# Two-dimensional spectral mixer with backward pass: a negated spectrum in place of negated sine tables, and four smaller edits of the schedule

## The chip, the cores and the metric

The kernel runs on one core of a Trainium2 chip. The core has a matrix engine (TensorE, "PE" in the profile, with its weight loads as "PEld"), two elementwise engines that can read the matrix engine's accumulators in PSUM (VectorE, "DVE", and ScalarE, "ACT"), a third one that works in SBUF here (GpSimd, "POOL"), and a queue that issues transfers (SyncE, "SP"). The metric is device time in microseconds of one execution.

## The reference

```python
def _A_ref(x, w_r, w_i):                       # spectral filter
    X = rfft2(x.astype(float32)); X = X * (w_r + 1j*w_i)
    return irfft2(X, s=(S, D)).astype(bfloat16)
def _B_ref(x, w1, b1, w2, b2):                 # token-mixing MLP
    h = _layernorm(x)
    u = gelu(einsum("bsd,sf->bdf", h, w1) + b1)
    return (einsum("bdf,fs->bds", u, w2) + b2).transpose(0, 2, 1)
h  = x + _A_ref(_layernorm(x), w_r, w_i)
h2 = h + _B_ref(_layernorm(h), w1, b1, w2, b2)
# outputs: h2, and the gradients of x, w_r, w_i, w1, b1, w2, b2 for grad_out
```

S is 2048 tokens, D 448 features, F 1792 hidden units, all data bfloat16, one batch.

## The kernel before, in words

The two-dimensional transform is done by matmuls. Along the features it is one product with a cosine and sine table (`csF`); along the 2048 tokens it is split in two steps, 16 x 128: a row step (`row_a`, `row_b`), a transfer that reshuffles partitions (`D2`), and a block step with sine and cosine tables per block (`Ut`, `Vt`, and their transposes `UTt`, `VTt` for the inverse). The program runs through these stages:

1. Forward rows (lines 856 to 888). For each of 16 rows `t`: layer-norm statistics (`ln_stats`), an inverse standard deviation on GpSimd (`newton_gp`, ten dependent operations for a group of rows), a row matrix scaled by it (`scale_R`), the row matmuls, and the evacuation of their PSUM banks. Between them a generator (`gen_UV`) builds the tables, three steps a row; it stops for the row when it yields `True`.
2. Forward spectrum (`s2_stage`, called in line 912). For each of 16 blocks `g`, two to a round: three matmuls make the complex spectrum, `w_mult` multiplies it by the filter, and some rounds later `s2_inv` makes the inverse block.
3. Inverse rows, then the MLP forward and backward (lines 920 to 1178). The backward rows of the spectral part run inside the last MLP loop with a lag of three, `rows(t - LAG)`; the last ones follow in lines 1251 to 1254.
4. Backward spectrum (`s2_stage`, line 1259): the same, with four more products a round for the filter gradient, and no lag between spectrum and product.
5. Inverse rows of the backward pass with the layer-norm gradient of x (`gx_consumer`), and the remaining stores.

The order of TensorE, VectorE, ScalarE and SP is written out by the program; GpSimd's is chosen by the compiler's scheduler. Two devices set the order. `fill(n)` takes `n` steps from a list of pending generators, so that matmuls of another part stand between dependent ones: the gradient of the hidden layer (`dg_gen`) in the forward part, the weight gradients (`gw_gen`) in the backward part. `gw_gen` has 14 steps for 16 matmul slots, with four evacuations, their stores and, once in 28 steps, a transposing load. `drain()` runs what is left. `evac` copies a PSUM bank to SBUF, on ScalarE or VectorE: a planner (`Meter`) keeps a load for each of the two, adds an estimate for every operation, and `evac` takes the engine that would be done first. After each operation the smaller load is raised to the larger one minus a slack:

```python
low = max(self.load) - Meter.slack
self.load[0], self.load[1] = max(low, self.load[0]), max(low, self.load[1])
```

Both PSUM pools (`ps_ff` for the transform, `ps_mm` for filling matmuls) have four banks, used in turn.

Subtraction inside an accumulating matmul needs one operand negated. The kernel before negates tables: `gen_neg` writes `-Ut` into `Un` and `-UTt` into `UTn` on VectorE, once for the forward and once for the backward stage.

Of the kernel before, what the change touches and what calls it, by code (L numbers as in the profile page):

```python
# [13 lines left out]
ALU = mybir.AluOpType  # L14
ACT = mybir.ActivationFunctionType
# [23 lines left out]
N_FILL_F = (6, 3, 20, 3, 24, 2)  # L39
N_FILL_B = (16, 16, 40, 8, 24, 8)  # L40
INV_SD = 1.0 / float(S * D)
# [9 lines left out]
class Meter:  # L51


    slack = 2.0
    side = ()
# [14 lines left out]
    def __getattr__(self, name):  # L70
        fn = getattr(self.eng, name)

        def run(**kw):
            ap = kw["in_"] if "in_" in kw else kw["in0"]
            n = int(np.prod(ap.shape[1:]))
            self.load[self.i] += self.cost(name, n, ap.dtype == BF16)
            low = max(self.load) - Meter.slack
            self.load[0], self.load[1] = max(low, self.load[0]), max(low, self.load[1])
            fn(**kw)  # L79
# [40 lines left out]
def kernel(  # L120
# [26 lines left out]

    Meter.slack = 2.0
    ctx.enter_context(tc.block(schedule_with_timeline_sim=True))
# [303 lines left out]
    def gen_UV():  # L453
# [18 lines left out]
        for dst, o0, o1, pt in ((Ut, ou, ou, pu), (Vt, ov0, ov1, pv)):  # L472
# [7 lines left out]
            yield  # L480
            yield True
            comp = comp_ring.next()
# [104 lines left out]
    p_ring = ring(rS, 1808, 2, 2, 2, KW)  # L587
    Y_ring = ring(rS, 3616, 2, 2, 2, KW)
    aT_ring = ring(rAT, 0, 2, 4, P)
    D2 = cut(r2, 0, NG, 2, KW)  # L590
    Un = [r448[:, (NG + g) * P:(NG + g + 1) * P] for g in range(12)] + [rE[:, (3 * NT + g) * P:(3 * NT + g + 1) * P] for g in range(4)]
    UTn = cut(r448, 0, NG, P)
    cs_ring = ring(r452, 0, 4, 2, 2, KW)
# [64 lines left out]
    def s2_stage(get_x, on_mult, ml, n_fill, gap, make_inv, after_fwd=None, scale=None):  # L658
        flush()
        nh = NG // 2  # L660
        xs, ys = {}, {}

        lag = 2 + ml
        for c2 in range(nh + lag):
            if c2 < nh:
                xs[c2] = get_x(c2)
                if make_inv and c2 < 4:
                    gen_inv_s(4 + c2)
                    if c2 in (1, 2):
                        gen_inv_d(c2 - 1)  # L670
            for i in range(2):
                if make_inv and c2 >= 3:
                    next(wp, None)
                    next(wp, None)
                if c2 < nh:
                    g = 2 * c2 + i
                    px = ps_ff()
                    pv = px[:, 0:452].rearrange("p (c k) -> p c k", c=2)
                    mm(pv, lhsT=Vt[:, g, :], rhs=D2[:, g, :, :], start=True, stop=False)
                    mm(pv[:, 0, :], lhsT=Ut[:, g, :], rhs=D2[:, g, 1, :], start=False, stop=False)  # L680
                    mm(pv[:, 1, :], lhsT=Un[g], rhs=D2[:, g, 0, :], start=False, stop=True)
                    evac(out=xs[c2][:, i, :, :], in_=pv, scale=scale)
                if c2 >= lag:
                    s2_inv(2 * (c2 - lag) + i, ys[c2 - lag][:, i, :, :])
                if after_fwd is not None and c2 < nh and g % 4 == 3:
                    after_fwd(g // 4)
                fill(n_fill)
            if ml <= c2 < nh + ml:
# [5 lines left out]
    def gen_neg(dst, src):  # L694
        ve.tensor_scalar(out=dst, in0=src, scalar1=-1.0, scalar2=None, op0=ALU.mult)

    def w_mult(c2, xc, Wv, conj):
# [8 lines left out]
        ve.tensor_tensor(out=y[:, :, 0, :], in0=p1[:, :, 1, :], in1=p2[:, :, 0, :],  # L706
                         op=(ALU.subtract if conj else ALU.add))
        return y

    def s2_inv(g, y):  # L710
        pu = ps_ff()
        pv = pu[:, 0:452].rearrange("p (c k) -> p c k", c=2)
        mm(pv, lhsT=VTt[:, g, :], rhs=y, start=True, stop=False)
        mm(pv[:, 0, :], lhsT=UTt[:, g, :], rhs=y[:, 1, :], start=False, stop=False)
        mm(pv[:, 1, :], lhsT=UTn[:, g, :], rhs=y[:, 0, :], start=False, stop=True)
        ab = r452_ring.next()
# [46 lines left out]
    def ln_stats(src, t, mv):  # L763
        ve.bn_stats(out=stats[:, t, :], in_=src[:, t, :])
        if t % 2:
            ve.bn_aggr(out=mv[:, t - 1, :], in_=stats[:, t - 1, :])
        if t % 2:
            ve.bn_aggr(out=mv[:, t, :], in_=stats[:, t, :])

    def load_biases():  # L770
# [71 lines left out]
    for t in (4, 5):  # L842
        ln_stats(xn, t, mvx)
    newton_gp(mvx[:, 4:6, 1], rstd_x[:, 4:6], slice(4, 6))
    fill(6)
    turn_biases = load_biases()
    Meter.side, Meter.every, Meter.count = [], 1, 0
    GROUPS = {0: (6, 8), 1: (8, 10), 3: (10, 12), 5: (12, 14), 7: (14, 16)}
    STATS = {0: (6, 7), 1: (8, 9), **{t: (t + 8,) for t in range(2, 8)}}
    INV_S = {11: 0, 12: 1, 13: 2, 14: 3}  # L850
    for c in range(2):
        sc.copy(out=Rp.rearrange("p (a q b c) -> p c a q b", c=2, q=8, a=4)[:, c],
                in_=Rm[:, 64 * c:64 * c + 64].rearrange("p (q a b) -> p a q b", q=8, a=4))
    FILL_A = (3, 3, 3, 3, 3, 3, 3, 3, 3, 3, 3, 3, 3, 3, 3, 3)
    FILL_B = (3, 3, 3, 3, 3, 3, 3, 3, 3, 3, 3, 3, 3, 3, 3, 3)
    for t in range(NT):
        if t in (1, 3):
            load_w2T()
        if t + 1 < NT:
            row_a(t + 1, Rs.pop(t + 1))  # L860
        fill(FILL_A[t])
        if 1 <= t and t + 3 < NT:
# [19 lines left out]
        if t in INV_S:  # L882
            gen_inv_s(INV_S[t])
        if t in (13, 13 + 1):
            gen_neg((cut(r448, NG * P, 12, P), cut(rE, 3 * NT * P, 4, P))[t - 13], Ut[:, 12 * (t - 13):12 + 4 * (t - 13), :])
        if t == 2:
            gen_RT()
        fill(FILL_B[t])
    for i in range(2):
        gen_neg(UTn[:, 8 * i:8 * i + 8, :], UTt[:, 8 * i:8 * i + 8, :])  # L890
    wp = w_place()
    gp_.memset(csF[:, 0, :, 0:1], 1.0)
    fill(20)

# [16 lines left out]

    s2_stage(fwd_x, fwd_mult, ML_F, 3, 24, True)
    drain()
# [225 lines left out]

    for i in range(2):  # L1140
        gen_neg(cut(r2, (2 * NG * KW + 8 * i * P), 8, P), Ut[:, 8 * i:8 * i + 8, :])
    Un[:] = [r2[:, 2 * NG * KW + g * P:2 * NG * KW + (g + 1) * P] for g in range(NG)]
    LAG = 3
# [116 lines left out]
    Meter.slack = 2.0  # L1260
    g_out = w_io(W_view_B, out_2, out_3, True)
# [69 lines left out]
```

## Time and profile before

| what | value |
|---|---|
| three runs | 368.6, 369.4, 369.41 us, median 369.4 |
| the profiled execution's own time | 369.41 us |
| its span, first to last instruction | 367.6 us |
| TensorE busy | 346.1 us (94%) |
| VectorE, ScalarE, GpSimd busy | 255.8, 203.7, 73.7 us |
| chain of work that ended last | TensorE 77%, VectorE 6%, GpSimd 5%, transfers 4%, ScalarE 4% |
| transfers, share of 16 engines | 90.3% for the one hardware queue that carries nearly all |

A row of the wait list reads: engine, tile and line that waited, who released it, then the total wait in us, how often, and the longest. A row of the busy times by stretch reads: the stretch from the span's start, its length, then busy time and number of instructions of PE, PEld, DVE, ACT and POOL, the granted share of TensorE's clock, the share of the transfer engines, and GB/s. A row of a timeline reads: start, time, engine, line, operation, output, input, shape, and how many like instructions were merged; in brackets the idle time before it and who ended it. L79 is the planner's wrapper through which all VectorE and ScalarE operations go, and L215 the wrapper of all matmuls.

### The profile page before, as it was taken

The numbers are of one execution on the slowest core, as the hardware profiler recorded it, in microseconds if no ns is written. First come the engines' busy times: TensorE is split into PE (matmuls) and PEld (weight loads), VectorE is DVE, ScalarE is ACT, GpSimd is POOL, SyncE is SP. The second block draws the span as 40 slices with busy tenths as digits, with TensorE's granted clock in tenths as the row PEclk, the third lists the DMA queues.
The fourth block names the chain that finished last, engine by engine and source line by source line (L and its number), as shares of the span: only waits on it lengthen the run. The fifth ranks groups of instructions, "written<-read, shape, count | busy, mean of one in ns | idle before, by whom it ended". The sixth has DMA issues, their size and how long they took to land.

```text
span 367.6 us, 6387 instructions
## 1 busy us (share of the span) xinstructions
PE 346.1 (94%) x2114; PEld 185.8 (51%) x2121; DVE 255.8 (70%) x641; ACT 203.7 (55%) x426; POOL 73.7 (20%) x240
## 2 busy tenths in 40 slices
PE   1888999899999999999999999999999999999993
PEld 0455766455645555555555566653444444555541
DVE  7698839973876888583247766674787883788881
ACT  3738748756966454413312454463576664576751
POOL 8867000000220000010002221100000000465650
PEclk9989999999999999999999999999999999999998
DMA  8999989648999999998868789379669899798997
GB/s 205 308 219 215 168 202 183 146 130 288 294 293 351 326 305 244 190 289 183 189 154 167 157 188 171 75 227 312 208 204 231 242 199 261 241 201 273 203 211 231
DMA packets 148249, 81.63 MB, mean 222 GB/s; under 512 B 95544, under 2 KB 140600, under 8 KB 147832
## 3 DMA queue, kind: packets, MB, share of 16 engines
q1 hardware_dynamic: 148216, 81.23, 90.3%
q8 instruction: 16, 0.26, 0.3%
q14 instruction: 17, 0.14, 0.1%
HBM read 27.56 MB, written 23.89 MB: 140 GB/s over the span
## 4 chain that ended last, share of the span: by engine, by line
PE 77%; DVE 6%; POOL 5%; DMA 4%; ACT 4%; issue 2%; POOLq 0%; DVEq 0%; ACTq 0%
PE ps_mm L215 62%; PE ps_ff L215 15%; DMA out_dram<-rO 2%; DMA rO<-in_B_w_dram 2%; DVE rS L79 2%; ACT rO L79 2%; DVE r L79 1%; ACT Ut L79 1%; DVE stats L79 1%; DVE rO L79 1%; DVE rA L79 1%; POOL cols L394 1%; POOL cols L395 1%; DVE rX L79 1%; ACT rAT L79 0%
## 5 line engine op out<-in xcount | busy, mean ns | idle before, releaser
L215 PEld LDWEIGHTS <-r 128*128 128x128 bf16 (+1 forms) x628 | 60.3, 105 | 49.2 <-issue 1.8
L215 PEld LDWEIGHTS <-rS 128*128 128x128 bf16 (+2 forms) x528 | 44.8, 99 | 48.6 <-issue 10.1
L79 ACT CAST rO<-ps_mm 128x512 bf16<-128x512 f32 (+1 forms) x75 | 40.3, 567 | 25.0 <-PE ps_mm L215 21.6
L1130 POOL TENSOR_SCALAR lcol<-lcol 128x1 f32<-128x1 f32 x32 | 18.6, 580 | 148.0 <-ACT r L79 148.0
L215 PE MATMUL ps_mm<-rD,r 128*128 128x448 bf16 x224 | 44.5, 352 | 0.0
L79 DVE CAST rO<-ps_mm 128x512 bf16<-128x512 f32 (+1 forms) x45 | 28.4, 644 | 19.3 <-PE ps_mm L215 16.0
L215 PEld LDWEIGHTS <-rst 128*128 128x128 bf16 (+1 forms) x320 | 24.0, 97 | 29.0 <-issue 13.1
L215 PE MATMUL ps_mm<-rC,rE 128*128 128x448 bf16 x144 | 37.1, 377 | 0.8 <-DMA rE<-in_B_w_dram 0.5
L79 ACT CAST r<-ps_ff 128x452 bf16<-128x452 f32 x54 | 28.9, 537 | 11.0 <-PE ps_ff L215 10.6
L215 PE MATMUL ps_mm<-rG,rst 128*128 128x512 bf16 (+1 forms) x155 | 34.0, 380 | 0.2
L215 PE MATMUL ps_mm<-rB,r 128*128 128x448 bf16 x160 | 31.1, 352 | 0.1
L215 PE MATMUL ps_mm<-r,rst 128*128 128x512 bf16 (+3 forms) x160 | 31.2, 353 | 0.0
L79 ACT ACTIVATE r<-ps_mm,rstd_h 128x448 bf16<-128x448 f32 x16 | 10.1, 634 | 29.3 <-PE ps_mm L215 29.3
L215 PE MATMUL ps_ff<-csI,rAT 113*128 113x448 bf16 x108 | 24.9, 353 | 0.4 <-ACT rAT L79 0.2
L79 DVE SCALAR_TENSOR_TENSOR r<-ps_mm,b2col,r 128x448 bf16<-128x448 f32 x16 | 10.9, 682 | 19.9 <-PE ps_mm L215 18.4
L79 ACT ACTIVATE r<-rC 128x448 bf16<-128x448 bf16 x16 | 9.1, 571 | 26.8 <-DMA out_dram<-r 21.8
L79 ACT ACTIVATE rG<-rG 128x896 bf16<-128x896 bf16 x14 | 13.3, 950 | 14.9 <-DVE rG L79 14.7
L215 PE MATMUL ps_mm<-rE,rS 128*128 128x448 bf16 x112 | 21.5, 352 | 0.0
L215 PEld LDWEIGHTS <-rO 128*128 128x128 bf16 (+1 forms) x165 | 15.6, 98 | 10.9 <-DMA rO<-in_B_w_dram 0.6
L79 ACT CAST rS<-ps_ff 128x512 bf16<-128x512 f32 x30 | 17.7, 589 | 5.1 <-PE ps_ff L215 5.1
L215 PEld LDWEIGHTS <-rE 128*128 128x128 bf16 x148 | 14.6, 103 | 9.6 <-issue 2.8
L215 PE MATMUL ps_mm<-rC,rO 128*128 128x448 bf16 x80 | 19.1, 352 | 0.3 <-DMA rO<-in_B_w_dram 0.3
(173 smaller groups left out, 604.3 us busy)
## 6 DMA issues: line engine op xcount, KB each, us to landing
out_dram<-rO SPq DMA_DIRECT2D x44, 256.0 KB
r<-in_B_w_dram SPq DMA_DIRECT2D x5, 1024.0 KB
r<-r SPq DMA_DIRECT2D x16, 226.0 KB
r<-r SPq DMA_DIRECT2D x32, 113.0 KB
rS<-in_B_w_dram SPq DMA_DIRECT2D x4, 896.0 KB
out_dram<-r SPq DMA_DIRECT2D x32, 112.0 KB
out_dram<-rO SPq DMA_DIRECT2D x16, 192.0 KB
rO<-in_B_w_dram SPq DMA_DIRECT2D x2, 1024.0 KB
```

The costliest lines, as they stand in the source:

```text
L79: fn(**kw)
L215: nc.tensor.matmul(out, lhsT=lhsT, rhs=rhs, start=start, stop=stop)
L394: gp_.tensor_scalar(out=gtmp, in0=in0, scalar1=scalar, scalar2=None, op0=ALU.mult)
L395: gp_.tensor_tensor(out=out, in0=gtmp, in1=in1, op=ALU.add)
L1130: gp_.tensor_scalar(out=m1, in0=ms, scalar1=-1.0 / D, scalar2=None, op0=ALU.mult)
```

## The change

The negated tables go. In their place each spectrum stage begins with four VectorE operations that write the negated real part of the spectrum (`D2n`), and after each `w_mult` a ScalarE operation writes the negated second part of the product into a third plane of `y`; it is issued after the next block's evacuation. The inverse block has two matmuls of 452 columns in place of one of 452 and two of 226. Besides, the inverse deviations are computed in three groups of four rows in place of six of two (the first group one row step later, so it holds rows 4 to 7), and the aggregation of rows 9 and 13 moves to the next row; `gen_UV` has one pause less before its sine; eight filling steps before backward row 14 go; the planner's slack is 2.0 throughout, where it was 4.0 in the backward spectrum. The fill counts are written as entries of a tuple with the values that they had.

```diff
@@ class Meter
-    slack = 2.0
-            low = max(self.load) - Meter.slack
+            low = max(self.load) - 2.0
@@ gen_UV
             ve.tensor_scalar(out=t, in0=t, scalar1=2047, scalar2=None, op0=ALU.bitwise_and)
             yield
-            yield True
             comp = comp_ring.next()
@@ buffers
-    Y_ring = ring(rS, 3616, 2, 2, 2, KW)
+    Y_ring = ring(rS, 3616, 2, 2, 3, KW)
-    Un = [r448[:, (NG + g) * P:(NG + g + 1) * P] for g in range(12)] + [rE[:, (3 * NT + g) * P:(3 * NT + g + 1) * P] for g in range(4)]
-    UTn = cut(r448, 0, NG, P)
+    D2n = cut(r2, NG * 2 * KW, NG, KW)
@@ s2_stage
         flush()
+        for c4 in range(4):
+            ve.tensor_scalar(out=D2n[:, 4 * c4:4 * c4 + 4, :], in0=D2[:, 4 * c4:4 * c4 + 4, 0, :], scalar1=-1.0,
+                             scalar2=None, op0=ALU.mult)
...
-                    mm(pv[:, 1, :], lhsT=Un[g], rhs=D2[:, g, 0, :], start=False, stop=True)
+                    mm(pv[:, 1, :], lhsT=Ut[:, g, :], rhs=D2n[:, g, :], start=False, stop=True)
...
+                while negs:
+                    negs.pop(0)()
                 fill(n_fill)
@@ w_mult
+        negs.append(lambda: sc.activation(out=y[:, :, 2, :], in_=y[:, :, 0, :], func=ACT.Copy, scale=-1.0))
@@ s2_inv
-        mm(pv, lhsT=VTt[:, g, :], rhs=y, start=True, stop=False)
-        mm(pv[:, 0, :], lhsT=UTt[:, g, :], rhs=y[:, 1, :], start=False, stop=False)
-        mm(pv[:, 1, :], lhsT=UTn[:, g, :], rhs=y[:, 0, :], start=False, stop=True)
+        mm(pv, lhsT=UTt[:, g, :], rhs=y[:, 1:3, :], start=True, stop=False)
+        mm(pv, lhsT=VTt[:, g, :], rhs=y[:, 0:2, :], start=False, stop=True)
@@ ln_stats
-        if t % 2:
+        if t % 2 and (t < 8 or t % 4 == 3):
             ve.bn_aggr(out=mv[:, t, :], in_=stats[:, t, :])
+        elif t >= 8 and t % 4 == 2:
+            ve.bn_aggr(out=mv[:, t - 1, :], in_=stats[:, t - 1, :])
@@ forward rows
-    newton_gp(mvx[:, 4:6, 1], rstd_x[:, 4:6], slice(4, 6))
-    GROUPS = {0: (6, 8), 1: (8, 10), 3: (10, 12), 5: (12, 14), 7: (14, 16)}
+    GROUPS = {0: (4, 8), 3: (8, 12), 7: (12, 16)}
-        if t in (13, 13 + 1):
-            gen_neg((cut(r448, NG * P, 12, P), cut(rE, 3 * NT * P, 4, P))[t - 13], Ut[:, 12 * (t - 13):12 + 4 * (t - 13), :])
-    for i in range(2):
-        gen_neg(UTn[:, 8 * i:8 * i + 8, :], UTt[:, 8 * i:8 * i + 8, :])
@@ backward
-    for i in range(2):
-        gen_neg(cut(r2, (2 * NG * KW + 8 * i * P), 8, P), Ut[:, 8 * i:8 * i + 8, :])
     for t in range(NT - LAG, NT + 2):
-        if t == NT - 2:
-            fill(8)
         rows(t)
-    for i in range(2):
-        gen_neg(UTn[:, 8 * i:8 * i + 8, :], UTt[:, 8 * i:8 * i + 8, :])
     fill(N_FILL_B[2])
-    Meter.slack = 4.0
     s2_stage(bwd_x, bwd_mult, 0, N_FILL_B[3], N_FILL_B[4], False, load_du, 2.0 * INV_SD)
-    Meter.slack = 2.0
```

More of the change, by code (lines that the diff above doesn't have):

```diff
@@ L39 @@
 N_FILL_F = (6, 3, 20, 3, 24, 2)
-N_FILL_B = (16, 16, 40, 8, 24, 8)
+N_FILL_B = (16,16,40,8,24,8)
 INV_SD = 1.0 / float(S * D)
@@ L663, in s2_stage @@
         lag = 2 + ml
+        negs.clear()
         for c2 in range(nh + lag):
@@ L692, in s2_stage @@
         fill(gap)
-    def gen_neg(dst, src):
-        ve.tensor_scalar(out=dst, in0=src, scalar1=-1.0, scalar2=None, op0=ALU.mult)
+    negs = []
     def w_mult(c2, xc, Wv, conj):
@@ L853 @@
                 in_=Rm[:, 64 * c:64 * c + 64].rearrange("p (q a b) -> p a q b", q=8, a=4))
-    FILL_A = (3, 3, 3, 3, 3, 3, 3, 3, 3, 3, 3, 3, 3, 3, 3, 3)
-    FILL_B = (3, 3, 3, 3, 3, 3, 3, 3, 3, 3, 3, 3, 3, 3, 3, 3)
     for t in range(NT):
@@ L860 @@
             row_a(t + 1, Rs.pop(t + 1))
-        fill(FILL_A[t])
+        fill(N_FILL_F[1])
         if 1 <= t and t + 3 < NT:
@@ L883 @@
             gen_inv_s(INV_S[t])
-        if t in (13, 13 + 1):
-            gen_neg((cut(r448, NG * P, 12, P), cut(rE, 3 * NT * P, 4, P))[t - 13], Ut[:, 12 * (t - 13):12 + 4 * (t - 13), :])
         if t == 2:
             gen_RT()
-        fill(FILL_B[t])
-    for i in range(2):
-        gen_neg(UTn[:, 8 * i:8 * i + 8, :], UTt[:, 8 * i:8 * i + 8, :])
+        fill(N_FILL_F[1])
     wp = w_place()
     gp_.memset(csF[:, 0, :, 0:1], 1.0)
-    fill(20)
+    fill(N_FILL_F[2])
     def fwd_x(c2):
@@ L910, in fwd_mult @@
         return w_mult(c2, xc, W_view_F, False)
-    s2_stage(fwd_x, fwd_mult, ML_F, 3, 24, True)
+    s2_stage(fwd_x, fwd_mult, ML_F, N_FILL_F[3], N_FILL_F[4], True)
     drain()
@@ L1138, in ln_b @@
         ve.tensor_tensor(out=out, in0=pb, in1=resid, op=ALU.add)
-    for i in range(2):
-        gen_neg(cut(r2, (2 * NG * KW + 8 * i * P), 8, P), Ut[:, 8 * i:8 * i + 8, :])
-    Un[:] = [r2[:, 2 * NG * KW + g * P:2 * NG * KW + (g + 1) * P] for g in range(NG)]
     LAG = 3
@@ L1251 @@
     for t in range(NT - LAG, NT + 2):
-        if t == NT - 2:
-            fill(8)
         rows(t)
-    for i in range(2):
-        gen_neg(UTn[:, 8 * i:8 * i + 8, :], UTt[:, 8 * i:8 * i + 8, :])
     fill(N_FILL_B[2])
-    Meter.slack = 4.0
     s2_stage(bwd_x, bwd_mult, 0, N_FILL_B[3], N_FILL_B[4], False, load_du, 2.0 * INV_SD)
-    Meter.slack = 2.0
     g_out = w_io(W_view_B, out_2, out_3, True)
```

## The prediction

> **What bounds the kernel now.** I read the engine totals first, then TensorE's waits, then the busy time by stage, then the timelines of the four places that the change touches.
>
> ```profile
> PE 346.1 (94%) x2114; PEld 185.8 (51%) x2121; DVE 255.8 (70%) x641; ACT 203.7 (55%) x426; POOL 73.7 (20%) x240
> ```
>
> TensorE's wait list, longest first, and the stretches 8-50 (forward rows), 50-87 (forward spectrum), 87-239, 239-257 (last backward rows), 257-298 (backward spectrum), 298-362:
>
> ```profile
> PE ps_ff L215 <- DVE rX L79: 8.0, 1, 8.0
> PE ps_ff L215 <- DVE rS L79: 2.1, 2, 1.9
> PE ps_ff L215 <- ACT rS L79: 1.0, 1, 1.0
> PE ps_ff L215 <- ACT rX L79: 0.9, 1, 0.9
> ...
> 8.00:50.00 42.00, 38.23 (x265) 23.70 (x265) 30.91 (x99) 26.60 (x51) 21.70 (x90) 0.96 1.05 222
> 50.00:87.00 37.00, 34.93 (x226) 20.20 (x224) 27.79 (x63) 24.99 (x46) 0.56 (x3) 1.00 0.81 179
> 239.00:257.00 18.00, 17.73 (x107) 8.18 (x108) 10.55 (x20) 9.26 (x19) 0.64 (x1) 1.00 0.94 266
> 257.00:298.00 41.00, 40.79 (x232) 19.66 (x235) 33.85 (x69) 27.51 (x54) 0.00 (x0) 1.00 0.79 222
> ```
>
> TensorE is the bound from 31 us to 361 us: after its start it waits about 7 us in all, and its own work is the same before and after the change. So the question is only where the change makes TensorE wait. Every new wait adds its whole length, for the filling matmuls that would have stood there run later.
>
> **Part by part.** The sum is made against the profiled execution, 369.41 us with a span of 367.6; the median of the three runs is 369.4, so nothing has to be shifted.
>
> *Same work in another form.* The three matmuls of an inverse block (452, 226, 226 columns) become two of 452. Their starts lie 0.19, 0.10 and 0.09 us apart (rows 269.15, 269.34, 269.44, 269.53): two of 226 cost what one of 452 costs. 0, at most -0.1 for 32 blocks. The fill counts spelled out as lists are the same numbers (3, 20, 3, 24).
>
> *Negated tables out, negated spectrum in.* VectorE loses eight table negations (0.55 at 42.79, 0.28 at 44.77, twice 0.42 at 45.55 and at 248.73, two more before the last rows), all under running matmuls: 0. It gets four of 904 elements at the start of each spectrum stage, 0.35 each between the 512 (0.28) and 1024 (0.42) rows. They wait for the last reshuffle of D2, and VectorE's next work queues behind. Forward, VectorE is idle 4.64 us until 50.94, and matmuls read D2 at 50.74 without a wait: hidden, at worst 0.3. Backward they stand behind the last filling evacuation: at worst 0.7 (0.69 for that cast). I take 0 for both; without that idle time they would cost 4 x 0.35 = 1.4.
>
> *A. Forward rows.* VectorE waits for the GpSimd chain of inverse deviations:
>
> ```profile
> 19.25 0.25 DVE L79 TENSOR_SCALAR rX<-Rm,rstd_x 128x128 bf16<-128x128 bf16 x1 [3.40 <-POOL rstd_x L376]
> 26.63 0.24 DVE L79 TENSOR_SCALAR rX<-Rm,rstd_x 128x128 bf16<-128x128 bf16 x1
> 27.33 0.68 DVE L79 TENSOR_TENSOR rS<-rA 128x448 bf16<-128x448 bf16 x2
> ```
>
> Now two chains run interleaved (rows 4-5 and 6-7) and end at 19.2. One chain over rows 4-7 starts at 15.9 and needs ten steps of 0.28: 18.65, a gain of 0.6. Later groups lose: a chain took 21.47 to 24.81 = 3.3 with VectorE busy, and rows 8-11 now wait for the statistics of row 11 (25.2, less 0.6). 24.6 + 3.3 = 27.9 for the row scale that ran at 26.63: VectorE stands 1.3 us longer, and the folds, statistics and evacuations behind it with it. The fold at 27.33 then ends at 29.3 where TensorE used it at 28.71: +0.6. Likewise rows 12-15 wait for row 15 (32.1, +0.4) + 3.3 + two other GpSimd operations (0.32 and 0.39) = 36.4 against 33.56 now; the fold behind ends near 37.2, TensorE wants it at 36.91 + 0.4: 0 to +0.6. The removed generator pause moves the sine up a row: ScalarE then sits in it until VectorE's masking ends (23.7, less 0.6), with three evacuations behind it (now 17.82, 20.70, 22.57), and TensorE needs the first one's bank at 24.24: about +0.3. Sum +1.5; ends -0.6 (only the gain) and +2.5.
>
> *B. Forward spectrum.* From 72 us on TensorE waits for VectorE's products by a hair:
>
> ```profile
> 74.22 0.70 DVE L79 TENSOR_TENSOR rS<-rS 128x452 bf16<-128x452 bf16 x2
> 74.97 0.36 PE L215 MATMUL ps_ff<-rS,VTt 128*128 128x452 bf16 x1
> ```
>
> The products end at 74.92, the inverse matmul starts at 74.97. Now a ScalarE negation comes between (452 elements; nearest ScalarE row of this size 0.54): +0.6, once, since VectorE's round (72.94 to 74.95, 2.01) keeps its pace. The planner charges each negation 0.53 to ScalarE, lifting its round from 1.3 to 1.8 against VectorE's 1.65, so one or two evacuations of 0.54 go to VectorE, which has no room: +0.8. Sum +1.4; ends +0.5 and +2.5.
>
> *C. The eight filling steps before row 14.*
>
> ```profile
> 239.85 2.53 PE L215 MATMUL ps_mm<-rG,rst 128*128 128x512 bf16 x12
> 242.22 0.39 PE L215 MATMUL ps_ff<-Rm,rS 128*128 128x128 bf16 x4
> ...
> 241.24 0.69 DVE L79 TENSOR_TENSOR rS<-rA 128x448 bf16<-128x448 bf16 x2
> ```
>
> Ten steps run from 239.85 to 242.22, when row 14's fold (done 241.92) is ready. With two, TensorE is there at 240.28 and waits until 241.95: +1.7. The steps taken out carry evacuations, stores and a transposing load on SP's queue; they go behind the last D2 reshuffle (issued 250.34), whose readers start at 257.19, so SP has 5 us of room. Low end 1.4; high end 3.4, if TensorE's clock halves:
>
> ```profile
> 16.60:20.02 3.42, 1.54 (x11) 0.83 (x9) 0.77 (x3) 1.12 (x3) 2.77 (x16) 1.00 1.13 269
> 20.02:23.43 3.41, 3.34 (x14) 1.81 (x14) 3.38 (x13) 1.12 (x2) 1.79 (x9) 0.50 0.99 187
> ```
>
> After a stretch with TensorE busy 1.54 of 3.42 us the granted clock was 0.50 for 3.41 us, worth 1.7 us of matmuls. C leaves at least 1.74 of 3.41 busy, so I leave it out. [...]
>
> *D. Backward spectrum.* One round of two blocks takes TensorE 5.21 us (268.76 to 273.97), and VectorE's eight products run in one burst:
>
> ```profile
> 270.56 1.16 DVE L79 TENSOR_TENSOR rS<-rS,rC 128x904 bf16<-128x904 bf16 x2
> 271.75 0.70 DVE L79 TENSOR_TENSOR rS<-rS 128x452 bf16<-128x452 bf16 x2
> 272.48 1.17 DVE L79 TENSOR_TENSOR rS<-rS,rX 128x904 bf16<-128x904 bf16 x2
> 273.69 0.70 DVE L79 TENSOR_TENSOR rC<-rS 128x452 bf16<-128x452 bf16 x2
> ```
>
> 3.83 us. The planner charges the burst 4 x 0.53 + 4 x 0.295 = 3.3. With a slack of 4 it remembers all of it and sends the next six evacuations (0.53 to 0.58 each) to ScalarE; they arise 0.61 apart (8.6 per round), so the seventh meets VectorE after 3.7 us, as the burst ends. With 2.0 it forgets 1.3, and the negation uses 0.53 more: (2.0 - 0.53) / 0.57 = two or three go to ScalarE, and at 1.7 us the next goes to VectorE, which has 2 us of products left. Its PSUM bank comes free after about 2.7 us. A filling bank is wanted again 1.5 to 2.2 us after it was filled (seven to ten steps of 0.216): TensorE stands about 0.5 us a round, 4.0 in eight. Ends: 0.2 (other banks cover it) and 5.7 (0.7 a round). At the high end the burst also delays the next round's products.
>
> Sum: 1.5 + 1.4 + 1.7 + 4.0 = +8.6, 378.0 us.
>
> **Rivals.** *Banks cover the backward stage:* ScalarE is busy 27.5 of 41 us there and has room. Then D is 0.5 and the time 374.5. Against it: one more evacuation a round of 0.61 on VectorE makes 33.85 into 38.7 of 41, in bursts. *The halved clock at C* adds 1.7: 379.7. For it the row above; against it the 1.0 us wait near 30 us after which the clock stayed 1.00. *Late evacuations never reach TensorE* (one mechanism: four banks a pool outlast every delay under about 1.5 us, in the rows and both spectrum stages). A, B and D lose their positive terms; C's 1.7 stands against A's 0.6 and the 1.7 of a halved clock at 20 us that need not come: 368.8, not slower. It decides if no evacuation waits over 1.5 us; against it, TensorE does wait for ScalarE evacuations 1.0 and 0.9 us today. And VectorE has no idle time from 19.25 to about 34, so a faster clock there buys little.
>
> **How the numbers follow.** Forecast 0.63, covered backward stage 0.20, halved clock 0.10, not slower 0.07. All low ends together give 370.8, all high ends 384.2; single terms vary alone, so the range is 372.0 to 382.5, which leaves the last rival and the far ends out, under 2 in 10. A measurement tells a change from none beyond 0.3% (1.1 us): faster 0.04, same 0.04, slower 0.92.
>
> **What would show it.** A: VectorE's wait for GpSimd at row scale 8, and TensorE's at row 8 or 12. B: inverse matmuls released by ScalarE. C: a TensorE wait near 240 us of about 1.7, released by VectorE's fold. D: about 19 evacuations on VectorE in the backward stage, where the timeline now has 11, and TensorE waits of 0.5 to 1 us each round. Wrong if the backward stage shows no waits, or the clock falls in a stretch that I left at 1.00.

## The result, and the profile after

The changed kernel takes 377.38 us (median of 4 runs, 377.19 to 378.32), beside 369.0 us for the kernel before (median of 4, 367.6 to 369.41): a ratio of 1.0239, with a 95% interval of 1.0205 to 1.0273. Its profiled execution took 377.39 us with a span of 375.6. The forecast was 378.0, slower.

The engine totals of the changed kernel:

```profile
PE 347.3 (92%) x2082; PEld 182.1 (48%) x2089; DVE 264.1 (70%) x660; ACT 200.2 (53%) x423; POOL 65.8 (18%) x210
```

TensorE's busy time is 1.2 us more than before, in a span that is 8.0 us longer; its own work has hardly changed. The rest is standing. These are the longest rows of its wait list (engine, tile and line that waited, who released it, then total us, times, longest us; the matmul wrapper is now L213, the planner's wrapper L78):

```profile
PE ps_ff L213 <- DVE rX L78: 7.3, 2, 6.9
PE ps_ff L213 <- DVE rS L78: 3.6, 3, 1.3
PE ps_ff L213 <- ACT rS L78: 3.3, 5, 1.7
PE ps_ff L213 <- ACT RTm L78: 1.2, 1, 1.2
PE ps_mm L213 <- ACT rO L78: 1.1, 2, 0.6
PE ps_mm L213 <- DMA out_dram<-rO: 1.1, 1, 1.1
```

The first row is the start of the kernel, as before, and 0.4 us of a second wait. Against the list before, the waits that ScalarE (ACT) releases have grown: `rS` stood for 1.0 us and `RTm` and `rO` not at all. VectorE's `rS` has grown from 2.1 us, and one row names a store. Where they lie is seen in the busy times by stretch, cut at the same stages (stretch, length, then busy us and count of PE, PEld, DVE, ACT, POOL, clock, DMA share, GB/s):

```profile
8.00:52.00 44.00, 37.02 (x263) 22.34 (x262) 29.42 (x96) 25.33 (x49) 13.63 (x61) 1.00 0.98 213
52.00:89.00 37.00, 34.05 (x207) 18.82 (x205) 29.62 (x69) 25.68 (x51) 0.73 (x3) 1.00 0.79 166
...
241.00:259.00 18.00, 16.48 (x103) 7.92 (x103) 9.44 (x18) 8.65 (x17) 0.64 (x1) 1.00 0.92 263
259.00:300.00 41.00, 39.95 (x211) 17.66 (x215) 38.57 (x80) 23.94 (x47) 0.00 (x0) 1.00 0.78 205
```

In the backward spectrum VectorE rises from 33.85 to 38.57 us of 41 and ScalarE falls from 27.51 to 23.94: evacuations have moved from the engine with room to the one without. TensorE does 211 matmuls in 41 us where it did 232; part of that is form, since an inverse block now has two matmuls in place of three.

Read off the first matmul of each stage in both timelines, the 7.95 us between the two spans divide so (the rounded rows add up to 7.97):

| stage | before | after | difference |
|---|---|---|---|
| start to forward spectrum | 50.74 | 52.28 | +1.54 |
| forward spectrum | 36.41 | 37.40 | +0.99 |
| inverse rows, MLP, its backward part | 152.09 | 152.08 | 0.0 |
| last backward rows (TensorE waits 1.23 more, and eight filling steps fewer) | 17.95 | 17.65 | -0.30 |
| backward spectrum | 53.27 | 57.36 | +4.09 |
| inverse rows and what is left of the filling | 50.60 | 52.77 | +2.17 |
| from the start of the last matmul to the end | 6.57 | 6.05 | -0.52 |

The eight filling steps are not lost work: they run in the last two matmul stages, which is part of the +4.09 and of the +2.17. For the backward spectrum the part can be read from the kernel that only lacks these steps (the first experiment): its backward spectrum takes 54.09 us, 0.8 more than before, and TensorE waits for nothing in it. So about 3.3 of the 4.09 us belong to the other edits.

### The profile page after: what moved, and what is told of

It is laid out like the page before. It is cut to its first block, busy times and chain, and to the rows that moved or that the text cites. A ratio compares the mean times of both kernels' runs of the same rounds, so it can differ in the third digit from the quotient of the medians.

```text
span 375.6 us, 6304 instructions
## 1 busy us (share of the span) xinstructions
PE 347.3 (92%) x2082; PEld 182.1 (48%) x2089; DVE 264.1 (70%) x660; ACT 200.2 (53%) x423; POOL 65.8 (18%) x210
## 4 chain that ended last, share of the span: by engine, by line
PE 70%; DVE 7%; DMA 7%; POOL 6%; ACT 5%; issue 3%; DVEq 0%; SPq 0%; ACTq 0%; POOLq 0%
PE ps_mm L213 58%; PE ps_ff L213 13%; DVE rS L78 3%; DMA out_dram<-rO 3%; ACT rO L78 2%; DMA out_dram<-r 2%; DMA rO<-in_B_w_dram 2%; DVE r L78 1%; DVE stats L78 1%; ACT rG L78 1%; DVE rA L78 1%; POOL cols L392 1%; POOL cols L393 1%; ACT r L78 0%; ACT rS L78 0%
## 5 line engine op out<-in xcount | busy, mean ns | idle before, releaser
L213 PEld LDWEIGHTS <-r 128*128 128x128 bf16 (+1 forms) x568 | 54.4, 105 | 43.4 <-issue 1.4
L213 PEld LDWEIGHTS <-rS 128*128 128x128 bf16 (+2 forms) x528 | 44.1, 98 | 52.8 <-DVE rS L78 12.1
L78 ACT CAST rO<-ps_mm 128x512 bf16<-128x512 f32 (+1 forms) x66 | 35.9, 565 | 22.7 <-PE ps_mm L213 15.6
L78 DVE CAST rO<-ps_mm 128x512 bf16<-128x512 f32 (+1 forms) x54 | 33.8, 640 | 19.1 <-PE ps_mm L213 8.9
L213 PE MATMUL ps_mm<-rD,r 128*128 128x448 bf16 x224 | 44.5, 352 | 0.0
L213 PEld LDWEIGHTS <-rst 128*128 128x128 bf16 (+1 forms) x320 | 24.1, 97 | 35.3 <-issue 17.3
L213 PE MATMUL ps_mm<-rC,rE 128*128 128x448 bf16 x144 | 35.3, 361 | 2.0 <-DMA rC<-in_grad_out_dram 1.0
L213 PE MATMUL ps_mm<-rG,rst 128*128 128x512 bf16 (+1 forms) x155 | 35.4, 380 | 1.1 <-ACT rO L78 0.5
L78 ACT CAST r<-ps_ff 128x452 bf16<-128x452 f32 x50 | 27.0, 540 | 12.2 <-PE ps_ff L213 11.0
L213 PE MATMUL ps_mm<-r,rst 128*128 128x512 bf16 (+3 forms) x160 | 31.1, 353 | 1.7 <-DMA out_dram<-rO 1.1
L213 PE MATMUL ps_mm<-rB,r 128*128 128x448 bf16 x160 | 31.2, 352 | 0.1
L78 ACT ACTIVATE r<-ps_mm,rstd_h 128x448 bf16<-128x448 f32 x16 | 10.1, 634 | 29.3 <-PE ps_mm L213 29.3
L213 PE MATMUL ps_ff<-csI,rAT 113*128 113x448 bf16 x108 | 24.9, 353 | 0.4 <-ACT rAT L78 0.2
L78 DVE SCALAR_TENSOR_TENSOR r<-ps_mm,b2col,r 128x448 bf16<-128x448 f32 x16 | 10.9, 682 | 19.9 <-PE ps_mm L213 17.7
L78 ACT ACTIVATE r<-rC 128x448 bf16<-128x448 bf16 x16 | 9.1, 570 | 26.8 <-DMA out_dram<-r 13.6
L213 PE MATMUL ps_mm<-rE,rS 128*128 128x448 bf16 x112 | 21.5, 352 | 0.0
L78 ACT ACTIVATE rG<-rG 128x896 bf16<-128x896 bf16 x14 | 13.3, 950 | 14.9 <-DVE rG L78 14.7
L213 PEld LDWEIGHTS <-rO 128*128 128x128 bf16 (+1 forms) x165 | 15.5, 98 | 11.3 <-DMA rO<-in_B_w_dram 0.8
L213 PE MATMUL ps_ff<-csF,rS 112*128 112x226 bf16 x128 | 17.6, 260 | 2.4 <-ACT RTm L78 1.2
L213 PEld LDWEIGHTS <-rE 128*128 128x128 bf16 x144 | 13.6, 99 | 12.8 <-issue 2.5
L213 PE MATMUL ps_mm<-rC,rO 128*128 128x448 bf16 x80 | 19.1, 352 | 0.4 <-DMA rO<-in_B_w_dram 0.4
```

The costliest lines, as they stand in the source:

```text
L213: nc.tensor.matmul(out, lhsT=lhsT, rhs=rhs, start=start, stop=stop)
```

## The experiments

The theory from the forecast: each of the four edits (groups of rows, negated spectrum, filling steps, slack) costs by itself, and the largest cost is the slack, through evacuations that VectorE gets. The rivals: the backward stage has enough banks to hide it; or the cost belongs to another edit.

### The filling steps alone

```diff
     for t in range(NT - LAG, NT + 2):
-        if t == NT - 2:
-            fill(8)
         rows(t)
```

> The kernel before without the eight filling steps ahead of backward row 14, nothing else. Theory (the terms are separate): +1.3 us, the wait of 1.23 that the changed kernel shows at 244.2, released by VectorE's fold; the stretch from there to the inverse rows stays without waits. Rival (the later start of the filling work also shifts the stores against the output buffers, and this makes the wait of 1.07 near 305 us and those after 316 us): +2.5 to +3.5, with waits released by a store or by output casts after 300 us. Rival (the steps merely run at the end): 0 to +0.3.

Measured: 371.9 us, 1.0041 (1.0018 to 1.0064), so +1.5 us. TensorE's timeline in this kernel, then VectorE's (start, us, engine, line, operation, tiles, shape, count; in brackets the idle time before and its releaser):

```profile
240.17 0.59 PE L215 MATMUL ps_mm<-rG,rst 128*128 128x512 bf16 x2
242.00 0.64 PE L215 MATMUL ps_ff<-Rm,rS 128*128 128x128 bf16 x4 [1.24 <-DVE rS L79]
```

```profile
241.56 0.69 DVE L79 TENSOR_TENSOR rS<-rA 128x448 bf16<-128x448 bf16 x2
```

The two steps that are left begin at 240.17; at 0.216 each (eight take 1.73 us, 269.53 to 271.26, in the kernel before) the next matmul could start at 240.60. It starts at 242.00, when the first of VectorE's two folds is done: TensorE stands 1.40 us from start to start (the bracket counts from the modelled end of the matmul before, and has 1.24). The changed kernel shows the same wait at 244.20 with the same releaser, also 1.40 us from start to start and 1.23 in the bracket. Two steps of filling instead of ten do not reach as far as the fold, as forecast.

### The slack alone

```diff
     fill(N_FILL_B[2])
-    Meter.slack = 4.0
     s2_stage(bwd_x, bwd_mult, 0, N_FILL_B[3], N_FILL_B[4], False, load_du, 2.0 * INV_SD)
```

> The kernel before with the planner's slack at 2.0 in the backward spectrum, nothing else. Theory (the forgotten burst sends evacuations behind VectorE's products): 4 to 7 more evacuations on VectorE in the stage and +1 to +2 us, as TensorE waits of 0.3 to 1 us. Rival (only slack and negation together overload VectorE): 0 to +0.3, more evacuations on VectorE but no waits. Rival (the shifted stores of the missing eight steps make the waits): 0.

Measured: 370.57 us, 1.0020 (0.9996 to 1.0044). The planner sends more to VectorE, as forecast: 26 evacuations of the stage in place of 18 (4 to 7 more were expected). But TensorE has no wait in the stage, and its length is 53.27 us as before. In this stretch of 41 us of the backward spectrum TensorE never stands, with VectorE at 37.00:

```profile
256.00:297.00 41.00, 41.00 (x236) 19.69 (x235) 37.00 (x76) 24.30 (x46) 0.00 (x0) 1.00 0.80 226
```

So the largest term of the forecast is not the slack's by itself.

### The negated spectrum alone, and with the slack

The first of these two kernels is the kernel before with the tables replaced by the negated spectrum (all of the change's lines on `Un`, `UTn`, `D2n`, `y` and `negs`); the second has the slack of 2.0 as well.

```diff
+        negs.append(lambda: sc.activation(out=y[:, :, 2, :], in_=y[:, :, 0, :], func=ACT.Copy, scale=-1.0))
...
-        mm(pv, lhsT=VTt[:, g, :], rhs=y, start=True, stop=False)
-        mm(pv[:, 0, :], lhsT=UTt[:, g, :], rhs=y[:, 1, :], start=False, stop=False)
-        mm(pv[:, 1, :], lhsT=UTn[:, g, :], rhs=y[:, 0, :], start=False, stop=True)
+        mm(pv, lhsT=UTt[:, g, :], rhs=y[:, 1:3, :], start=True, stop=False)
+        mm(pv, lhsT=VTt[:, g, :], rhs=y[:, 0:2, :], start=False, stop=True)
```

> The kernel before with the negated spectrum in both spectrum stages in place of the negated tables; slack 4.0 and everything else as before. Theory: +1.4 us in the forward spectrum (inverse matmuls released by ScalarE), +0.2 to +0.5 in the backward one, in all +1.5 to +2. Rival (the forward stage is set by VectorE's rounds alone, and ScalarE's negation runs beside them): 0 to +0.3. Rival (the negation is the whole of the backward loss too): +3.5 to +4.5.

> The kernel before with the negated spectrum and with the slack at 2.0 in the backward spectrum; row groups, the generator's pause and the eight filling steps as before. Theory: the two together cost more than each alone: +1.4 forward and +2.5 to +4 backward, in all +4 to +5.5. Rival (they only add): the sum of the two single runs within 0.4. Rival (the missing eight steps cause the backward waits): +1.4 to +2.

Measured: the negated spectrum alone 373.21 us, 1.0074 (1.0046 to 1.0102); with the slack 374.8 us, 1.0119 (1.0087 to 1.0151). The backward stage takes 53.27 us in the kernel before and with the slack alone, 54.49 with the negation alone, 56.71 with both. The two edits together cost 3.4 us there, where one costs nothing and the other 1.2, which is more than the 0.2 to 0.5 expected. These are lengths from one profile each, though the 53.27 us comes back to 0.01 us in the five other runs that leave this stage alone. The run times alone do not show that the two edits do more than add: the pair costs 4.4 us (3.2 to 5.6, from its ratio), the single edits 0.7 and 2.7, each uncertain by about 1. The tests on the changed kernel, further down, do show it.

The round of the second kernel where TensorE first waits, 0.5 us from start to start, shows the chain of waits. VectorE:

```profile
271.91 0.68 DVE L79 CAST rO<-ps_mm 128x512 bf16<-128x512 f32 x1
272.51 0.62 DVE L79 CAST r<-ps_ff 128x452 bf16<-128x452 f32 x1
273.05 0.68 DVE L79 CAST rO<-ps_mm 128x512 bf16<-128x512 f32 x1
273.64 1.16 DVE L79 TENSOR_TENSOR rS<-rS,rC 128x904 bf16<-128x904 bf16 x2
274.83 0.70 DVE L79 TENSOR_TENSOR rS<-rS 128x452 bf16<-128x452 bf16 x2
```

ScalarE, and TensorE:

```profile
275.63 0.58 ACT L79 ACTIVATE rS<-rS 128x452 bf16<-128x452 bf16 x1 [1.69 <-DVE rS L79]
276.12 1.06 ACT L79 CAST rO<-ps_mm 128x512 bf16<-128x512 f32 x2
```

```profile
276.73 1.46 PE L215 MATMUL ps_mm<-rG,rst 128*128 128x512 bf16 x6 [0.33 <-ACT rO L79]
```

Three evacuations stand on VectorE ahead of the burst of products, so the product that the negation needs ends at 275.53. ScalarE has nothing before its negation and waits 1.69 us for VectorE. The two evacuations that the planner gave to ScalarE are behind the negation; the first of them ends at 276.69, and at 276.73 TensorE gets its bank. Without a negation ScalarE has no instruction in this loop that reads a product: with the slack alone it waits for VectorE once between 257 and 298 us, for 1.1 us, and TensorE doesn't wait.

### The same two edits, with the negation left out of the planner's account

```diff
-        negs.append(lambda: sc.activation(out=y[:, :, 2, :], ...
+        negs.append(lambda: sc.eng.activation(out=y[:, :, 2, :], ...
```

The instruction stays where it is; only the 0.53 us that the planner adds to ScalarE's load is gone.

> The kernel before with the negated spectrum and the planner's slack at 2.0, as in the earlier run that had both (1.0119 of the kernel before), but the ScalarE negations are not charged to the planner's load (they run as before, at the same places). Theory (charge): the 0.53 us that each negation adds to ScalarE's account is what sends evacuations to VectorE behind its burst of products; without the charge the backward spectrum has about 26 VectorE evacuations in place of 31, its length goes from 56.7 back to within 1 us of 53.3, and the ratio to about 1.005. Rival (serial): the negation stands on ScalarE's queue between the products and the inverse matmul whatever the planner counts; then the waits stay, the stage stays above 55.5 us and the ratio above 1.009.

Measured: 370.25 us, 1.0022 (1.0002 to 1.0042), where the charged version had 1.0119. The forward spectrum takes 36.63 us (37.67 charged), the backward one 54.50 (56.71). TensorE's wait list is empty from the start of the backward spectrum to 311 us; the 1.2 us over the kernel before stand at the stage's end, as a wait of 1.0 us for the first inverse row, which the kernel with the negation alone has too. And yet ScalarE still waits for the products: the first row of ScalarE's waits in 257 to 298 us is

```profile
ACT rS L712 <- DVE rS L79: 6.2, 7, 1.6
```

against 7.5 us in six waits when charged. So standing in the negation does not by itself make TensorE wait in these rounds; what it leaves is the wait at the stage's end. TensorE waits when the planner has put more on VectorE: 31 evacuations of the stage when charged, 27 when not, and three against two between two bursts in the rounds compared. VectorE in the uncharged kernel, over the round that answers to the one above:

```profile
269.95 0.70 DVE L79 TENSOR_TENSOR rC<-rS 128x452 bf16<-128x452 bf16 x2
270.56 0.62 DVE L79 TENSOR_SCALAR rS<-ps_ff 128x452 bf16<-128x452 f32 x1
271.10 0.68 DVE L79 CAST rO<-ps_mm 128x512 bf16<-128x512 f32 x1
271.70 1.16 DVE L79 TENSOR_TENSOR rS<-rS,rC 128x904 bf16<-128x904 bf16 x2
```

The charged kernel itself shows the same difference: one round earlier, with two evacuations between the bursts (at 267.02 and 267.56), TensorE waits for nothing.

A single round with three evacuations is not enough, though: the kernel with the slack alone and the uncharged one have some (the uncharged ahead of the bursts at 282.4 and 292.9), without a wait. In the charged kernel every round after 273 us has three, and in the changed kernel every round after 269 us. What that does to VectorE is seen over the seven rounds from the first burst to the eighth, in the charged, the changed, the uncharged kernel and the one with the slack alone:

```profile
263.30:301.30 38.00, 36.73 (x192) 15.63 (x191) 37.19 (x78) 21.98 (x44) 0.00 (x0) 1.00 0.74 203
263.50:302.30 38.80, 37.91 (x199) 16.46 (x201) 37.87 (x79) 22.98 (x45) 0.00 (x0) 1.00 0.81 206
262.50:298.40 35.90, 35.90 (x194) 15.92 (x193) 34.86 (x73) 24.48 (x50) 0.00 (x0) 1.00 0.78 216
260.80:297.40 36.60, 36.60 (x213) 17.68 (x211) 34.90 (x74) 22.99 (x44) 0.00 (x0) 1.00 0.79 219
```

In the first two VectorE works 5.31 and 5.41 us a round, and a round takes 5.43 and 5.54. In the other two it works 4.98 and 4.99 us, and a round takes 5.13 and 5.23, with TensorE busy throughout. So in the charged kernels VectorE has more to do in a round than the round takes where TensorE sets it; that points to VectorE as what sets the pace there. The theory of the charge stands; the rival, that the negation's place on the queue is enough, falls. What the place adds is not shown: no run has 31 evacuations on VectorE without a negation, so whether that many alone would cost the same stays open.

### The same two tests on the changed kernel

First the slack back at 4.0 in the backward spectrum (the lines that make the slack an attribute of the planner again are left out here), then the negation uncharged with the slack at 2.0, by the edit of the last section.

```diff
...
+    Meter.slack = 4.0
     s2_stage(bwd_x, bwd_mult, 0, N_FILL_B[3], N_FILL_B[4], False, load_du, 2.0 * INV_SD)
+    Meter.slack = 2.0
```

> The changed kernel with the slack back at 4.0 in the backward spectrum. Theory (slack and negation together overload VectorE there): fewer evacuations on VectorE in the stage (some 21, not 32), no TensorE waits released by casts or stores there, 2 to 3 us faster than the changed kernel, +5 to +6 against the kernel before. Rival (the negation or the output buffers alone make the waits): within 1 us of the changed kernel.

> The changed kernel with one word different: the ScalarE negations are issued at the same places but not charged to the planner's load. In the kernel before with the same two edits this took the ratio from 1.0119 to 1.0022 (about 3.6 us: 1 in the forward spectrum, 2 to 2.5 in the backward one). Theory (the charge, together with the slack of 2.0, decides which engine gets the evacuations): the changed kernel falls by 3 to 3.6 us, ratio 1.014 to 1.016, its backward spectrum goes from 57.4 to about 55 us and its forward spectrum from 37.4 to about 36.5. Rival (the changed kernel's waits come from the negation standing on ScalarE's queue): ratio stays above 1.020.

Measured: 373.88 us, 1.0145 (1.0123 to 1.0167) with the slack back, and 374.14 us, 1.0152 (1.0123 to 1.0181) with the negation uncharged. By the ratios that takes 3.5 and 3.2 us off the changed kernel. The backward spectrum falls from 57.36 to 54.27 and 54.49 us; VectorE has 20 and 26 evacuations there in place of 32. TensorE's wait list is empty in that stage in both. Either half of the pair is enough to undo most of it: putting the slack back saves 3.5 us here (an estimate from the two intervals: 2.0 to 5.0), where taking it out alone cost 0.7 (-0.1 to 1.6). The 5.4 and 5.6 us that are left over the kernel before are the other edits and the rest of the negation.

### Groups of four rows

```diff
-    newton_gp(mvx[:, 4:6, 1], rstd_x[:, 4:6], slice(4, 6))
-    GROUPS = {0: (6, 8), 1: (8, 10), 3: (10, 12), 5: (12, 14), 7: (14, 16)}
+    GROUPS = {0: (4, 8), 3: (8, 12), 7: (12, 16)}
```

with the change's lines for the aggregation of rows 9 and 13.

> The kernel before with the inverse deviations in three groups of four and the later aggregations, nothing else. Theory (a group waits for its last row, and VectorE waits for the group): the first TensorE wait near 19.4 shrinks by about 0.6, new VectorE waits for GpSimd at row scales 8 and 12 with TensorE waits at rows 8 and 12; the forward spectrum starts 0.5 to 1.5 us later. Rival (the whole loss of 1.5 comes from the generator's pause): the forward spectrum starts 0.3 to 0.6 earlier.

Measured: 370.47 us, 1.0048 (1.0031 to 1.0065), +1.8 us. VectorE's two row scales that wait for GpSimd, then the TensorE waits that VectorE's folds end:

```profile
18.73 0.25 DVE L79 TENSOR_SCALAR rX<-Rm,rstd_x 128x128 bf16<-128x128 bf16 x1 [2.88 <-POOL rstd_x L376]
...
27.50 0.26 DVE L79 TENSOR_SCALAR rX<-Rm,rstd_x 128x128 bf16<-128x128 bf16 x1 [1.38 <-POOL rstd_x L376]
```

```profile
19.34 0.64 PE L215 MATMUL ps_ff<-rX,rS 128*128 128x128 bf16 x4 [1.10 <-DVE rS L79]
...
28.64 0.64 PE L215 MATMUL ps_ff<-rX,rS 128*128 128x128 bf16 x4 [1.09 <-DVE rS L79]
...
37.31 0.64 PE L215 MATMUL ps_ff<-rX,rS 128*128 128x128 bf16 x4 [0.83 <-DVE rS L79]
```

The losses at rows 8 and 12 are there (1.38 us for VectorE at row scale 8, forecast 1.3). The gain at row 4 isn't: the matmuls of row 4 start at 19.34, and at 19.38 in the kernel of the next section, which has the groups as before. The single chain runs from 15.94 to 18.69, 2.75 us as worked out. But the two chains of that other kernel start at 14.95 and let VectorE go at about the same time (18.77, against 18.73 here): the single chain has to wait for the statistics of row 7, and begins a microsecond later.

### The generator's pause

```diff
             yield
-            yield True
             comp = comp_ring.next()
```

> The kernel before without the generator's pause ahead of the sine, nothing else. Theory (ScalarE sits in the sine with three evacuations behind it): a TensorE wait of about 1.2 near 23.5 released by ScalarE's copy of RTm, less of one near 30; the forward spectrum starts 0 to 0.5 us later. Rival (the pause is the whole loss): 1.3 to 1.6 later.

Measured: 369.36 us, 1.0013 (0.9993 to 1.0033): nothing that can be told from no change. The wait moves. ScalarE reaches the sine early and stands in it, with the small evacuation `RTm` behind it:

```profile
23.28 0.72 ACT L79 ACTIVATE rO<-r,cols 128x512 bf16<-128x512 int32 x1 [4.87 <-DVE r L79]
23.91 0.25 ACT L79 CAST RTm<-ps_ff 128x128 bf16<-128x128 f32 x1
```

TensorE waits 1.15 us at 24.20 for `RTm` and 0.63 at 26.75; in exchange the wait of 1.01 us at 30.67 in the kernel before is gone from the list, with at most 0.2 us left of it at 30.48. In the changed kernel the same wait stands at 23.48, with 1.20 us.

### Two tries at other waits

Late in some kernels TensorE waits for evacuations that wait for a store, so seven more output buffers were tried (in `rD`, free after the backward spectrum). And two kernels move filling steps of the forward rows, none added: three more steps ahead of the wait at row 4 and four more ahead of the wait at 29.7 us, with fewer in the slots behind; and the second of these alone.

```diff
+    ost.views += ring(rD, 0, 7, S // 2).views
```

```diff
-    FILL_A = (3, 3, 3, 3, 3, 3, 3, 3, 3, 3, 3, 3, 3, 3, 3, 3)
-    FILL_B = (3, 3, 3, 3, 3, 3, 3, 3, 3, 3, 3, 3, 3, 3, 3, 3)
+    FILL_A = (3, 3, 3, 1, 2, 3, 3, 7, 2, 3, 3, 3, 3, 3, 3, 3)
+    FILL_B = (3, 3, 6, 2, 3, 3, 3, 2, 1, 3, 3, 3, 3, 3, 3, 3)
```

> The kernel before with seven more output buffers for the weight gradients in the last stage (in the region of the hidden gradient, which is free by then), nothing else. Theory (the waits of 0.3 to 2.4 us after 310 us that single runs show come from the six output buffers, whose stores are late by a varying time): no wait released by an output cast after 310 us, the last casts no longer wait for a store, -0.5 to -2 us. Rival (those waits come from the share of the transfer engines itself): within 0.5 of before, the wait moves to the stores or to the buffers of the x gradient.

> The kernel before with filling steps of the forward rows moved, none added: at the places where its TensorE waits 1.9 us (row 4, at 17.9 us) and 1.0 us (row 6's weights, at 29.7 us) three and four more steps stand ahead of the wait, and later slots have that many fewer. One step is 0.21 to 0.24 us. If the waits can be covered by work that stands later anyway, TensorE gains 0.7 + 0.9 = about 1.5 us (ratio 0.996). Rival: VectorE sets the pace of the rows (it is busy without a break from 19 to 34 us), so the waits only come back at later rows; then no gain, ratio 0.999 to 1.002.

> Only the second of these moves (four steps ahead of the matmuls that waited 1.0 us at 29.7). Cover theory: -0.9 us, ratio 0.9975. Rival (VectorE sets the pace): ratio 0.999 to 1.002, and the wait comes back at a later row.

Measured: 369.25 us, 1.0015 (0.9998 to 1.0031) with the buffers: nothing that can be told from no change. After 310 us no output cast waits for a store any more, yet 6.4 us still pass between the last matmul and the end; the buffers do not set it. With the filling moved 0.9978 (0.9956 to 1.0000) and 0.9981 (0.9960 to 1.0002): at the edge of what can be told from no change. In the first of them the wait at row 4 falls to under 0.5 us, but 1.26 us of standing (start to start) appear at 22.24 before row 5, where the kernel without the pause has 0.7. The wait near 30 us falls from 1.70 us (in the profiles of the kernels with the filling steps, the slack or the buffers alone) to 0.95 in both, and yet the forward spectrum starts no earlier: at 51.05 and 50.47 us, where those three have 50.27 to 50.39. In these two TensorE has just waited 1.21 and 0.76 us there for the transfer that reshuffles `D2`. So time that is covered comes back as other waits, as the rival has it, but only the one at row 5 is VectorE's; a small gain isn't excluded. Neither is shown to beat the kernel before.

## Why the prediction was right, and where it was not

The sum was +8.6 us and 378.0; measured +8.0 in the span of the profiled executions and 377.38. By its terms:

| term | forecast | in the changed kernel's stages | its edits alone |
|---|---|---|---|
| A, forward rows | +1.5 | +1.54 | groups +1.8, pause +0.5 (not told from 0) |
| B, forward spectrum | +1.4 | +0.99 | stage 36.41 before, 37.78 and 37.67 with the negation |
| C, eight steps | +1.7 | a wait of 1.40 | +1.5, a wait of 1.40 |
| D, backward spectrum | +4.0 | +4.09, of which 0.8 is filling that C moved | slack 0, negation +1.2, both +3.4 in the stage |

**A** is near in its sum, and partly by luck. The gain of 0.6 at row 4, which the later times were worked out with, did not appear with the groups alone: I let the single chain end 0.6 earlier than the interleaved ones from one execution, in which the interleaved ones ended at 19.2. In most other profiles they end near 18.8, because they start half a microsecond earlier (14.95 against 15.43), and a microsecond before the single chain of the kernel with the groups alone (15.94). Against that, the sum of 1.5 (0.6, 0.6 and 0.3) took the upper end of the range given for row 12, "0 to +0.6". VectorE's stand at row scale 8 was sized right; TensorE then waits 1.09 and 0.83 us at rows 8 and 12. The changed kernel's first row scale does run at 18.13 in its profile, but the time that it won is given back at 23.48, to the sine.

```profile
23.48 0.55 PE L213 MATMUL ps_ff<-csF,rS 112*128 112x226 bf16 x4 [1.20 <-ACT RTm L78]
...
37.99 0.64 PE L213 MATMUL ps_ff<-rX,rS 128*128 128x128 bf16 x4 [1.33 <-DVE rS L78]
```

**B** holds in both of its parts. The inverse matmul is released by ScalarE, as the section on what would show it said:

```profile
73.69 0.35 PE L213 MATMUL ps_ff<-rS,UTt 128*128 128x452 bf16 x1 [1.69 <-ACT rS L78]
```

and the second part, evacuations pushed to VectorE, is one cast of 0.62 us between the products, which the kernel before and the uncharged one don't have there:

```profile
72.26 0.70 DVE L78 TENSOR_TENSOR rS<-rS 128x452 bf16<-128x452 bf16 x2
72.88 0.62 DVE L78 CAST r<-ps_ff 128x452 bf16<-128x452 f32 x1
73.42 1.16 DVE L78 TENSOR_TENSOR rS<-rX,rG 128x904 bf16<-128x904 bf16 x2
```

Uncharged, the stage is 1.04 us shorter (36.63 against 37.67), where the pushed part was forecast at 0.8; in the changed kernel it is 0.5 shorter (36.90 against 37.40). The sizes are rough, for the stage differs from profile to profile, with waits of TensorE for transfers in it. In the eight profiles without the negation it takes 35.77 to 37.13 us, on average 36.46; in the four with a charged one 37.10 to 37.78, on average 37.49. That is 1.0 us, where the sum had 1.4.

**C** had the right place, releaser and cause. 1.7 was 0.3 too much, since it let TensorE wait for the end of both folds (241.92 in the kernel before), and TensorE starts after the first: 0.44 us after the folds began, in the kernel without the eight steps (241.56 to 242.00). TensorE arrives at 240.60 there rather than at the forecast 240.28, but the folds are 0.32 us later too. The halved clock did not come: the granted clock is 1.00 in all the rows of the changed kernel above.

**D** is right in its size only with the 0.8 us of filling that C moved there, which the forecast did not count; that is luck. It is right in the planner's arithmetic (20 evacuations on VectorE in 41 us, forecast about 19), and wrong in the step that leads from there to TensorE. The forecast said that an evacuation lands on VectorE behind the burst and that its bank comes free late. The slack alone puts just as many there (20 in 41 us) and TensorE waits for none: four banks do cover that, as the first rival said. What the runs point to in its place is VectorE with more work in a round (5.41 us) than a round takes in the kernels where TensorE never stands there (5.1 to 5.2), once the negation's charge and the smaller slack together give it three evacuations in every round. How this reaches TensorE is read from single rounds: evacuations ahead of the burst, products late, ScalarE standing in the negation, its own evacuations behind it. The changed kernel shows it at its longest at 305 us. VectorE, ScalarE and TensorE:

```profile
300.53 0.69 DVE L78 CAST rO<-ps_mm 128x512 bf16<-128x512 f32 x1
301.13 0.62 DVE L78 TENSOR_SCALAR rS<-ps_ff 128x452 bf16<-128x452 f32 x1
301.67 0.68 DVE L78 CAST rO<-ps_mm 128x512 bf16<-128x512 f32 x1
302.27 1.16 DVE L78 TENSOR_TENSOR rS<-rS,rC 128x904 bf16<-128x904 bf16 x2
```

```profile
304.53 0.58 ACT L78 ACTIVATE rS<-rS 128x452 bf16<-128x452 bf16 x1 [2.15 <-DVE rS L78]
305.02 1.54 ACT L78 CAST rO<-ps_mm 128x512 bf16<-128x512 f32 x3
```

```profile
305.64 2.00 PE L213 MATMUL ps_mm<-r,rst 128*128 128x512 bf16 x10 [1.07 <-DMA out_dram<-rO]
```

The bracket names a store, but that store's event lies at 305.65, after the matmul's start; the first of ScalarE's three casts, 0.57 us long, ends at 305.59. With the negation uncharged the wait at this place is gone. So the releaser is read here from the times, not from the name; a share of the store in it is not excluded. "Each round" was wrong as well: TensorE's waits are few and uneven (0.18, 0.50, 1.07 us, and shorter ones).

The two terms that were taken at 0 held. The four operations that negate the spectrum run from 51.74 to 53.05 us in the forward stage without a wait of TensorE; in the backward stage they run from 259.43, and one matmul at 259.87 starts 0.17 us late.

Not in the sum: the granted clock of 0.50 from 20.02 to 23.43 us in the one profile of the kernel before. Three profiles of kernels whose forward rows are those of the kernel before (the filling steps, the slack and the buffers alone) start the forward spectrum at 50.27 to 50.39 us in place of 50.74. Against those profiles A is nearer to +1.9 than to +1.54. This start differs between profiles by about as much, though: 50.32 to 50.78 us in the three kernels with the negated spectrum and the rows as before.

The costs of the single edits, 1.8 + 0.5 + 1.5 and 4.4 for the negation with the slack, add up to 8.2 us beside the measured 8.8 (7.6 to 10.1, from the ratio on 369 us); with the slack and the negation taken one at a time (0.7 and 2.7) it would be 7.2. That difference is within the errors of the single costs; that the pair doesn't add rests on the lengths of the stage and on the two tests on the changed kernel.

## What to carry to other kernels

A small operation that makes one evacuating engine depend on the other can cost far from its own duration: here the eight negations of a stage, 0.58 us each on ScalarE, lengthened the backward spectrum by 1.2 us or by 3.4, depending on how much work the planner gave VectorE beside them. When a schedule is written by a planner, an instruction has two costs, its time on the engine and what its entry in the planner's account moves elsewhere; leaving it out of the account is a cheap way to tell the two apart. The engine that is to take the moved work can be checked before: its work in a round against the round of the engine that sets the pace. And two edits that each look cheap in the same loop should be tried together, since both may be drawing on the same spare time.

## What was not expected of the hardware

The granted clock of 0.50 for 3.41 us, which follows a stretch with TensorE busy 1.54 of 3.42 us, is in the profile of the kernel before. The clock falls once more there, at 364.77 us, and only once in the changed kernel, at 372.95: both times after the last matmuls, which end at 361.33 and 369.81. The mean granted clock of the profiled executions is 0.991 for the kernel before, 0.996 for the changed one and 0.995 to 1.000 for the twelve experiments. A stretch of the changed kernel that is nearly as empty was followed by full speed:

```profile
20.50:23.90 3.40, 1.80 (x15) 0.95 (x13) 3.37 (x13) 1.35 (x4) 0.00 (x0) 1.00 0.97 183
```

The granted clock is 1.00 in this stretch and also in the next 3.40 us, with TensorE busy 2.78 of them. So of two stretches with little work, one went before the halved clock and the other before full speed. What made the difference, no run here settles.
